# A spectral filter ahead of expert routing: the first two batches' last stage fed through DRAM instead of through transposes

## The chip, the cores and the metric

The kernel runs on one core of a Trainium2 chip. The metric is the device time of one execution in microseconds (us). A core has a matrix engine (TensorE, "PE" in the profile; "PEld" are its weight loads), VectorE (DVE), ScalarE (ACT), GpSimd (POOL) and a sync engine (SP) that issues most of the transfers. "SPq" and "ACTq" are the instruction queues of SP and ACT as issuers of DMAs. Each engine works through its instructions in the order in which the program issued them.

## The reference

All data is float32. `x` has 8 batches of 2496 tokens with 256 channels.

```python
X = np.fft.rfft(x, axis=1)
Y = X * (filt_r + 1j * filt_i)[None]
y = np.fft.irfft(Y, n=2496, axis=1)            # (8, 2496, 256)
t = y.reshape(19968, 256)
expert = token_ids * 2654435761 % 8
for e in range(8):
    rows = expert == e
    out[rows] = np.maximum(t[rows] @ w1[e], 0) @ w2[e]   # w1: 256 x 1024, w2: 1024 x 256
```

## The kernel before

**Two halves.** The transform along the 2496 = 39 x 64 tokens is made of matmuls, batch by batch. The second half gathers the filtered tokens by expert into tiles of 256 rows and runs each tile through its expert's two layers. A token of the first half is put to its place by a scatter: `stage3` copies its result into a tile `o` of 117 rows, and POOL issues one indirect DMA for each column of `o`, 22 for a batch, into the DRAM array `xs`. The tiles are loaded from `xs`. The first tiles hold tokens of batches 0 and 1, so they wait for every scatter of these two.

**The stages of a batch.** `stage1` is the 39-point transform: matmuls of `x` with the table `wf_t`, six steps of four columns (`u` = 0 to 5, the last one half as large). `forward` multiplies the result, in 20 planes of 128 partitions, two planes a step and so ten steps, by the table `d_t` and then, on VectorE, by the filter. `back` multiplies by the table `e_t`. `stage3` is the inverse 39-point transform with `wi_t`, again six steps of four columns, followed by four scatters a step (two in the last). `room` fills the columns of `o` that hold the token number. Between stages the data must change its partitions.

From batch 2 on it does so through DRAM: `stage1` stores to `d1`, `load2` loads from it, `back` stores to `d2`, `load4` loads from that. The first two batches differ. The first has no trip at all before its `forward` (`stage1_c`, `turn2`). And both of them have a `back_c` (L373) that makes the output with channels on the partitions, written into the buffer `self.out`, and a `turn4` (L382), which transposes this on TensorE, 44 transposes a batch, into the tile `t4` that `stage3` reads. The copies out of PSUM are ScalarE's for the first batch and VectorE's for the second.

**Buffers.** `self.out` of the first batch is the front part of `wts`, which later holds the weights of tiles 0 and 1 (`weights(0, .)` the first half of it, `weights(1, .)` the second). That of the second batch is `mid[:, 5:10]`, whose parts also serve as `stage1` output of the fourth batch. `t4` has two buffers, the tile `o` four (two pools, taken in turn), the input tiles `x` two; PSUM has four general banks (`fps`, tag "f") and four with names, a to d.

**The order.** The schedule is written by hand. Every piece of work is a pair of a number and a function; `todo` is sorted by the number, and the pieces are issued in that order. The numbers are roughly microseconds but they only order: nothing waits for a clock. `head` is the list of all that is issued before the first expert tile: batches 0 and 1 entirely, `stage1` of batch 2 (`third`) and two thirds of `stage1` of batch 3 (`fourth`), the routing, and the weights of tiles 0 and 1. The pieces of the later batches are issued between the steps of the expert tiles.

On SP's queue before the change stand, in this order: `load2` of the second batch (four of five groups), `load2` of the fifth, the third batch's x, the weights of tiles 0 and 1, the fourth batch's x, and then the first loads from `xs`. The third batch's `stage1` steps stand between the `turn4` and `stage3` steps of the second batch, the fourth's come after all of these:

```python
head += [(96 + 5 * u - 4 * (u > 0), lambda u=u: second.turn4(u)) for u in range(NU)]
head += [(98 + 5 * u, lambda u=u: second.stage3(u)) for u in range(NU)]
head += [(99 + 5 * u - 3 * (u == 5), lambda u=u: third.stage1(u)) for u in range(NU)]
head += [(123 + .1 * u, lambda u=u: fourth.stage1(u)) for u in range(4)]
```

Of the kernel before, what the change touches and what calls it, by code (L numbers as in the profile page):

```python
# [11 lines left out]
F32 = mybir.dt.float32  # L12
# [7 lines left out]
P = 128  # L20
B, S, C = 8, 2496, 256
# [8 lines left out]
NS, NQ = N1 // 2 + 1, 64  # L30
H, HN = 3, 21
H0 = (2 * HN, 0, HN)
NR = H * N1
NK = 2 * H * NS
SG = 4
XG = 4
NU = (HN + XG) // XG
XL = 2 * XG
# [87 lines left out]
def kernel(  # L126
# [10 lines left out]
    nc = tc.nc  # L137
# [17 lines left out]
    dpool = pool(ctx, "dram", 2, DRAM)  # L155
# [3 lines left out]
    t4pool = pool(ctx, "t4", 2)  # L159
    opool = pool(ctx, "op", 2)  # L160
    fps = pool(ctx, "fps", 4, PSUM)
    banks = {k: pool(ctx, f"bank_{k}", 1, PSUM) for k in "abcd"}

    ident = keep.tile([P, P], F32)
# [8 lines left out]
    e_t = cpool.tile([P, NS, P], F32)  # L173
# [45 lines left out]
    class Batch:  # L219


        def __init__(self, b):
            self.b = b
            self.d1 = self.d2 = None
            self.x, self.t2, self.t4, self.p, self.o = {}, {}, {}, {}, {}
            self.g = None
            if b < 2:

                if b == 0:
                    own = mid[:, 0:5, :].rearrange("p k f -> p (k f)")  # L230
                    self.mixed = own.rearrange("p (h n s) -> p h n s", h=2, s=NS)
                after = (held[:, 0:NS * C] if b == 0 else mid[:, 5:10, :].rearrange("p k f -> p (k f)"))
                self.out = after.rearrange("p (h n s) -> p h n s", h=2, s=NS)

        def load1(self, v):

# [16 lines left out]
        def products(self, w, rows, cols, src, dst, copy, u, name):  # L253


            last = XG * u + XG > HN
            for i in range(1 if last else XG // 2):
                ps = fps.tile([P, 2, C], F32, name=f"{name}_{self.b}_{u}_{i}", tag="f")
                if last:
                    for k, f in enumerate((H, 1)):  # L260
                        nc.tensor.matmul(out=ps[0:cols * f, k, :], lhsT=w[0:rows[k], 0:cols * f],
                                         rhs=src[0:rows[k], k, :], start=True, stop=True)
                    for k, f in enumerate((H, 1)):
                        copy(out=dst[0:cols * f, k, 0:C], in_=ps[0:cols * f, k, :])
                else:
                    for k in range(2):
                        nc.tensor.matmul(out=ps[0:cols * H, k, :], lhsT=w[:], rhs=src[:, 2 * i + k, :],  # L267
                                         start=True, stop=True)
                    copy(out=dst[:, 2 * i:2 * i + 2, 0:C], in_=ps[0:cols * H])  # L269
# [100 lines left out]
            self.t2[u] = held[:, a:a + 2 * C].rearrange("p (i c) -> p i c", c=C)  # L370
            nc.scalar.copy(out=self.t2[u], in_=ps[:])

        def back_c(self, u):  # L373
            pr = self.p.pop(u)
            ps = fps.tile([P, 2, 2, P], F32, name=f"pc_{self.b}_{u}", tag="f")
            for i in range(2):
                for h in range(2):
                    nc.tensor.matmul(out=ps[:, i, h, :], lhsT=pr[:, i, h * P:(h + 1) * P],
                                     rhs=e_t[:, 2 * u + i, :], start=True, stop=True)
            nc.scalar.copy(out=self.out[:, :, :, 2 * u:2 * u + 2], in_=ps[:].rearrange("p i h n -> p h n i"))  # L380

        def turn4(self, u):  # L382
            v, j0 = divmod(XG * u, XL)
            if j0 == 0:
                self.t4[v] = t4pool.tile([NK, XL, C], F32, name=f"t4_{self.b}_{v}", tag="t4")
            copy = nc.vector.tensor_copy if self.b else nc.scalar.copy
            for k in range(0, min(XG, HN + 1 - XG * u), 2):
                tag = ("bc" if self.b and u % 2 else "ad")[k // 2]
                ps = banks[tag].tile([P, 2, C], F32, name=f"pu_{self.b}_{u}_{k}", tag=tag)
                rows = [2 * NS * (H if XG * u + k + i < HN else 1) for i in range(2)]  # L390
                for i in range(2):
                    n0 = 2 * H * (XG * u + k + i)
                    for h in range(2):
                        nc.tensor.transpose(out=ps[0:rows[i], i, h * P:(h + 1) * P],
                                            in_=self.out[:, h].rearrange("p n s -> p (n s)")[:, n0 * NS:n0 * NS + rows[i]],
                                            identity=ident[:])
                if rows[0] == rows[1]:
                    copy(out=self.t4[v][:, j0 + k:j0 + k + 2, :], in_=ps[0:NK])
                else:
                    for i in range(2):  # L400
                        copy(out=self.t4[v][0:rows[i], j0 + k + i, :], in_=ps[0:rows[i], i, :])

        def load4(self, v):
            self.t4[v] = t4pool.tile([NK, XL, C], F32, name=f"t4_{self.b}_{v}", tag="t4")
# [36 lines left out]
    first, second = batches[:2]  # L441
# [307 lines left out]
    N_2 = NS // 2  # L749

    def chain(k):

        for step, j in ((Batch.turn2, k + 1), (Batch.back_c, k - 2), (Batch.forward, k)):
            if 0 <= j < N_2:
                step(first, j)

# [6 lines left out]
    third = batches[2]  # L763
# [10 lines left out]
    head += [(30.1, lambda: nc.sync.dma_start(out=wi_t[:], in_=wi_dram.ap()))]  # L774
    head += [(t, lambda u=u: second.stage1(u)) for u, t in enumerate((27, 32, 38, 41, 45, 48.5))]
    head += [(15, places), (64, tile_experts), (70, experts), (118, blanks)]
    head += [(t, lambda g=g: second.load2(g)) for g, t in enumerate((54, 54.1, 54.2, 54.3, 70))]
    head += [(62.7 + 2.9 * u, lambda u=u: second.forward(u)) for u in range(N_2)]
    head += [(62.7 + 2.9 * (u + 2) - .1, lambda u=u: second.back_c(u)) for u in range(N_2)]
    at = (63, 68.6, 74.4, 80.2, 86, 91)  # L780
    head += [(t, lambda u=u: first.room(u)) for u, t in enumerate((60, 65, 71, 77, 83, 88.5))]
    head += [(t, lambda u=u: second.room(u)) for u, t in enumerate((92, 96.9, 101.9, 106.9, 111.9, 116.9))]
    head += [(t, lambda u=u: first.turn4(u)) for u, t in enumerate(at)]
    head += [(t + 3, lambda u=u: first.stage3(u)) for u, t in enumerate(at)]
    head += [(t, lambda v=v: third.load1(v)) for v, t in enumerate((72, 73, 74))]
    head += [(t, lambda k=k: weights(k // 2, k % 2)) for k, t in enumerate((95, 95.1, 95.2, 95.3))]
    head += [(96 + 5 * u - 4 * (u > 0), lambda u=u: second.turn4(u)) for u in range(NU)]
    head += [(98 + 5 * u, lambda u=u: second.stage3(u)) for u in range(NU)]
    head += [(99 + 5 * u - 3 * (u == 5), lambda u=u: third.stage1(u)) for u in range(NU)]
    head += [(123.5, lambda: begin()), (123.6, lambda: [load(i) for i in range(2)])]  # L790
    head += [(124, lambda: [nc.sync.dma_start(out=dram, in_=chip) for dram, chip in put_off[2]])]
    head += [(125 + .1 * g, lambda g=g: third.load2(g)) for g in range(4)]
    fourth = batches[3]
    head += [(126, lambda: [nc.sync.dma_start(out=dram, in_=chip) for dram, chip in put_off[3]])]
    head += [(t, lambda v=v: fourth.load1(v)) for v, t in enumerate((113, 113.1))]
    head += [(123 + .1 * u, lambda u=u: fourth.stage1(u)) for u in range(4)]
    todo = [(t - 200, piece) for t, piece in head]
    todo += [(t, lambda k=k: pads(k)) for k, t in enumerate((10.9, 11.6, 11.9, 16.9, 17.6, 17.95, 22.9))]

# [331 lines left out]
```

## Time and profile before

| | |
|---|---|
| median of 3 runs | 1425.08 us (1418.89 to 1428.87) |
| the profiled execution | 1424.24 us, its span 1422.5 us |
| mean granted TensorE clock | 0.99 |
| first matmul of the first expert tile | 141.85 us from the span's start |
| last scatter of the second batch issued | 135.26 us |
| scatters (POOL, L433) in the whole kernel | 176, of 1006 ns on average |
| stage 3 matmuls `pd` (L267) in the whole kernel | 320, of 385 ns |

The span is the time from the first to the last recorded instruction. In a line of a timeline, the first column is the start, the second the duration from the first to the last of the merged instructions, then come engine, source line, operation, output and input, shapes, the count, and in brackets the idle time of the engine before it with what ended it. In the chain of waits, each line is a start, a duration and what was being waited for or done. A line of a table by stretches has, for each engine, the busy time and in brackets the number of instructions, and at the end the granted clock, the DMA engines' busy share and the GB/s. Busy times of TensorE are modelled ends of pipelined matmuls: a group of 8 that is listed with 1.89 us comes every 1.73.

### The profile page before, as it was taken

To read this page: it belongs to the slowest core of one execution; us is meant where nothing else is said; L and a number is where in the kernel's file an instruction comes from. 1 tells how busy PE (TensorE), PEld (TensorE's weight loads), DVE (VectorE), ACT (ScalarE), POOL (GpSimd) and SP (SyncE) were. 2 spreads that over 40 slices of the span, in tenths; PEclk is the share of its full clock that TensorE was granted. 3 is DMA by queue.
4 is the path that set the end of the run, shared out by engine and by line. 5 is a ranking of instruction groups with operands and counts; after the bars stand their busy time and mean duration, and the time that the engine had idled before them with its cause. 6 is when DMAs were issued, how large, how long until landed. Compare 5 with 4: busy or idle time off the path is not lost.

```text
span 1422.5 us, 26307 instructions
## 1 busy us (share of the span) xinstructions
PE 1373.4 (97%) x9398; PEld 1273.3 (90%) x9398; DVE 890.2 (63%) x1636; ACT 416.6 (29%) x760; POOL 830.3 (58%) x736
## 2 busy tenths in 40 slices
PE   7898999999999999999999999999999999999997
PEld 7776888989888988889999899999999999999997
DVE  7773575575556566445665477657766776676775
ACT  4554122223232223232222222222222222222222
POOL 6167243844665565578533587788855566555563
PEclk9999899999999999999999999999999999999999
DMA  8677765757987698888755785887742526261611
GB/s 222 206 235 216 212 218 121 260 192 245 269 270 224 183 284 264 261 262 273 241 167 131 219 258 170 235 242 235 254 138 68 190 62 199 46 218 42 215 46 35
DMA packets 244505, 278.33 MB, mean 196 GB/s; under 512 B 125171, under 2 KB 213670, under 8 KB 234948
## 3 DMA queue, kind: packets, MB, share of 16 engines
q1 hardware_dynamic: 95149, 179.33, 40.2%
q10 hardware_dynamic: 129303, 52.69, 15.4%
q0 software_dynamic: 19920, 44.59, 8.9%
q8 instruction: 77, 1.26, 0.4%
q14 instruction: 56, 0.46, 0.1%
HBM read 293.65 MB, written 86.15 MB: 267 GB/s over the span
## 4 chain that ended last, share of the span: by engine, by line
PE 86%; DMA 8%; DVE 3%; issue 1%; ACT 1%; ACTq 0%; SPq 0%; POOLq 0%; POOL 0%; DVEq 0%
PE dps L922 22%; PE up_b L887 9%; PE up_a L887 6%; PE up_c L887 6%; PE pd L267 5%; PE pb L312 4%; PE dnc L949 4%; PE dnb L949 4%; PE dna L949 4%; PE upc L944 4%; PE upa L944 4%; PE pc L335 3%; PE pa L267 3%; DMA t<-d 2%; PE upe L944 2%; PE upb L944 2%
## 5 line engine op out<-in xcount | busy, mean ns | idle before, releaser
L922 PE MATMUL dps<-wts,ht 128*128 128x256 f32 x1600 | 370.9, 382 | 6.1 <-ACT ht L891 6.1
L922 PEld LDWEIGHTS dps<-wts,ht 128*128 128x128 f32 x1600 | 304.7, 192 | 50.6 <-ACT ht L891 7.3
L1014 POOL DMA_INDIRECT out_dram<-osb,no x158 | 165.2, 1046 | 219.2 <-DVE osb L956 137.8
L433 POOL DMA_INDIRECT xs<-o,sidx x176 | 177.0, 1006 | 168.7 <-ACT o L269 73.3
L877 POOL TENSOR_TENSOR tw<-wts 128x512 f32<-128x512 f32 x158 | 205.1, 1298 | 116.0 <-DMA wts<-in_moe_w_dram 92.4
L877 POOL TENSOR_TENSOR tw<-wts,tw 128x512 f32<-128x512 f32 x158 | 206.1, 1305 | 6.2
L894 DVE TENSOR_TENSOR ht<-up_b,ht 128x512 f32<-128x512 f32 x150 | 103.7, 691 | 114.6 <-PE up_b L887 91.2
L891 ACT ACTIVATE ht<-ht 128x512 f32<-128x512 f32 x150 | 94.3, 630 | 188.8 <-DVE ht L894 164.9
L322 DVE TENSOR_TENSOR z<-pb,filt 64x512 f32<-64x512 f32 x160 | 110.2, 689 | 30.9 <-PE pc L335 28.9
L927 DVE COPY osb<-dps 128x512 f32<-128x512 f32 x50 | 34.6, 691 | 150.2 <-PE dps L922 149.7
L887 PE MATMUL up_a<-xt,wts 128*128 128x128 f32 x800 | 115.3, 277 | 9.1 <-DVE xt L855 4.9
L887 PEld LDWEIGHTS up_a<-xt,wts 128*128 128x128 f32 x800 | 105.9, 193 | 12.7 <-DVE xt L855 5.3
L887 PE MATMUL up_b<-st,tw 128*128 128x128 f32 x800 | 107.4, 278 | 2.7 <-DVE ht L894 1.8
L887 PEld LDWEIGHTS up_b<-st,tw 128*128 128x128 f32 x800 | 98.1, 193 | 4.9 <-issue 3.7
L953 ACT ACTIVATE ht<-ht 128x512 f32<-128x512 f32 x90 | 56.6, 630 | 122.1 <-DVE ht L956 75.8
L894 DVE TENSOR_TENSOR ht<-up_c,ht 128x512 f32<-128x512 f32 x100 | 69.0, 690 | 37.2 <-PE up_c L887 32.4
L338 ACT COPY mid<-pc 128x512 f32<-128x512 f32 x60 | 35.0, 584 | 154.8 <-PE pc L335 91.5
L267 PE MATMUL pd<-t,wi_t 120*117 120x256 f32 x320 | 77.5, 385 | 2.6 <-DMA t<-d 2.6
L318 DVE TENSOR_TENSOR y<-pb,filt 128x512 f32<-128x512 f32 x80 | 55.1, 689 | 37.8 <-PE pb L312 35.6
L269 ACT COPY o<-pd 117x512 f32<-117x512 f32 x80 | 45.0, 585 | 104.4 <-DMA xg<-xs 45.4
L312 PE MATMUL pb<-mid,d_t 128*128 128x256 f32 x280 | 74.1, 388 | 1.1 <-DVE z L322 1.1
L898 ACT COPY ht<-up_a 128x512 f32<-128x512 f32 x50 | 29.3, 587 | 150.6 <-PE up_a L887 120.7
(210 smaller groups left out, 2466.1 us busy)
## 6 DMA issues: line engine op xcount, KB each, us to landing
wts<-in_moe_w_dram SPq DMA_DIRECT2D x162, 1024.0 KB
xg<-xs ACTq DMA_DIRECT2D x321, 64.0 KB
mid<-d SPq DMA_DIRECT2D x70, 256.0 KB
d<-mid ACTq DMA_DIRECT2D x60, 256.0 KB
d_t<-t2s SPq DMA_DIRECT2D x15, 1024.0 KB
e_t<-t2s SPq DMA_DIRECT2D x15, 1024.0 KB
x<-in_x_dram SPq DMA_DIRECT2D x39, 312.0 KB
t<-d SPq DMA_DIRECT2D x12, 960.0 KB
```

Of the source, the lines that this page charges most:

```text
L267: nc.tensor.matmul(out=ps[0:cols * H, k, :], lhsT=w[:], rhs=src[:, 2 * i + k, :], start=True, stop=True)
L312: nc.tensor.matmul(out=ps[:, i, :], lhsT=d_t[:, s, :], rhs=rhs, start=True, stop=True)
L322: nc.vector.tensor_tensor(out=z[b], in0=ps[a], in1=f_t[1][64 * hi:64 * hi + 64, s1:s1 + 2, :], op=OP.mult)
L433: st = nc.gpsimd.indirect_dma_start(out=xs[:], out_offset=bass.IndirectOffsetOnAxis(ap=index, axis=0), in_=rows, in_offset=None, bounds_ch ...
L877: eng.tensor_tensor(t[k][:], p, q, op=OP.subtract)
L887: nc.tensor.matmul(out=ps[bank][:, f, :], lhsT=w[:, f * P:(f + 1) * P], rhs=xx, start=first and f == 0, stop=True, skip_group_check=True)
L891: nc.scalar.activation(out=out, in_=in_, func=AF.Relu)
L894: nc.vector.tensor_tensor(out, ps[bank][:], other, op=OP.add)
L922: nc.tensor.matmul(out=ps[:, h, :], lhsT=ht[:, h, fp, :], rhs=w2[:, fp, :], start=(fp == 0), stop=(fp == FP - 1))
L944: nc.tensor.matmul(out=ps[:, f, :], lhsT=w[:, f * P:(f + 1) * P], rhs=xx, start=first and f == 0, stop=True, skip_group_check=True)
L949: nc.tensor.matmul(out=ps[:, 0, :], lhsT=a[:, f, :], rhs=b[:, f, :], start=first and f == 0, stop=True, skip_group_check=True)
L1014: st = nc.gpsimd.indirect_dma_start(out=out[:], out_offset=bass.IndirectOffsetOnAxis(ap=to_rows[i][:, h:h + 1], axis=0), in_=o[:, h, :], i ...
```

## The change

For the first two batches `turn4` and `back_c` go. `back_on_chip` keeps the output in planes, as `back` does for later batches, and copies it into the same buffer `self.out`. `put` stores a fifth of it (four planes, 128 partitions x 4 KB) to a DRAM tile `d2`, right after the second `back_on_chip` of each fifth, and `fetch` loads a third of the columns from `d2` into the tile `t4` for `stage3`. Both are issued on SP. The first `fetch` of a batch follows its last `put` at once. `stage3` of the two batches uses the PSUM banks a to d.

The order in `head` is written anew. On SP now stand, one after another: four `put` of the first batch with four `load2` of the second ahead of the fifth `put`; `fetch` 0 and 1; the last `load2`; the third batch's x; `put` 0 of the second batch; the first batch's `fetch` 2; `put` 1; `weights(0, .)`; `put` 2, 3, 4; `fetch` 0 and 1 of the second batch; `fetch` 2; `weights(1, .)`; the fourth batch's x. On TensorE the third batch's `stage1` is issued about the end of the second batch's `back_on_chip` (four of its six steps after the last one, ahead of `stage3`(0)), and the fourth's steps between the `stage3` steps of the second.

```diff
             for i in range(1 if last else XG // 2):
-                ps = fps.tile([P, 2, C], F32, name=f"{name}_{self.b}_{u}_{i}", tag="f")
+                tag = ("bc" if u % 2 else "ad")[i] if name == "pd" and self.b < 2 else "f"
+                ps = (fps if tag == "f" else banks[tag]).tile([P, 2, C], F32, name=f"{name}_{self.b}_{u}_{i}", tag=tag)
...
-        def back_c(self, u):
+        def back_on_chip(self, u):
             pr = self.p.pop(u)
-            ps = fps.tile([P, 2, 2, P], F32, name=f"pc_{self.b}_{u}", tag="f")
+            ps = fps.tile([P, 2, C], F32, name=f"pc_{self.b}_{u}", tag="f")
             for i in range(2):
-                for h in range(2):
-                    nc.tensor.matmul(out=ps[:, i, h, :], lhsT=pr[:, i, h * P:(h + 1) * P],
-                                     rhs=e_t[:, 2 * u + i, :], start=True, stop=True)
-            nc.scalar.copy(out=self.out[:, :, :, 2 * u:2 * u + 2], in_=ps[:].rearrange("p i h n -> p h n i"))
-
-        def turn4(self, u):
...
+                nc.tensor.matmul(out=ps[:, i, :], lhsT=e_t[:, 2 * u + i, :], rhs=pr[:, i, :], start=True, stop=True)
+            nc.scalar.copy(out=self.out[:, 2 * u:2 * u + 2, :], in_=ps[:])
+
+        def put(self, k):
+
+            if self.d2 is None:
+                self.d2 = dpool.tile([P, NS, C], F32, name=f"d2_{self.b}", tag="d2")
+            sl = slice(SG * k, SG * k + SG)
+            nc.sync.dma_start(out=self.d2[:, sl, :], in_=self.out[:, sl, :])
+
+        def fetch(self, v):
+            t4 = self.t4[v] = t4pool.tile([NK, XL, C], F32, name=f"t4_{self.b}_{v}", tag="t4")
+            n = min(XL, HN - XL * v)
+            main = self.d2[0:2 * H * HN].rearrange("(j x) s c -> (x s) j c", x=2 * H)
+            nc.sync.dma_start(out=t4[:, 0:n, :], in_=main[:, XL * v:XL * v + n, :])
+            if n < XL:
+                nc.sync.dma_start(out=t4[0:2 * NS, n, :], in_=self.d2[2 * H * HN:P].rearrange("x s c -> (x s) c"))
...
-        for step, j in ((Batch.turn2, k + 1), (Batch.back_c, k - 2), (Batch.forward, k)):
+        for step, j in ((Batch.turn2, k + 1), (Batch.back_on_chip, k - 2), (Batch.forward, k)):
...
-    head += [(t, lambda g=g: second.load2(g)) for g, t in enumerate((54, 54.1, 54.2, 54.3, 70))]
+    head += [(t, lambda g=g: second.load2(g)) for g, t in enumerate((55.5, 55.6, 55.7, 55.8, 66))]
...
-    head += [(62.7 + 2.9 * (u + 2) - .1, lambda u=u: second.back_c(u)) for u in range(N_2)]
-    at = (63, 68.6, 74.4, 80.2, 86, 91)
-    head += [(t, lambda u=u: first.room(u)) for u, t in enumerate((60, 65, 71, 77, 83, 88.5))]
-    head += [(t, lambda u=u: second.room(u)) for u, t in enumerate((92, 96.9, 101.9, 106.9, 111.9, 116.9))]
-    head += [(t, lambda u=u: first.turn4(u)) for u, t in enumerate(at)]
-    head += [(t + 3, lambda u=u: first.stage3(u)) for u, t in enumerate(at)]
-    head += [(t, lambda v=v: third.load1(v)) for v, t in enumerate((72, 73, 74))]
-    head += [(t, lambda k=k: weights(k // 2, k % 2)) for k, t in enumerate((95, 95.1, 95.2, 95.3))]
-    head += [(96 + 5 * u - 4 * (u > 0), lambda u=u: second.turn4(u)) for u in range(NU)]
-    head += [(98 + 5 * u, lambda u=u: second.stage3(u)) for u in range(NU)]
-    head += [(99 + 5 * u - 3 * (u == 5), lambda u=u: third.stage1(u)) for u in range(NU)]
+    head += [(62.7 + 2.9 * (u + 2) - .1, lambda u=u: second.back_on_chip(u)) for u in range(N_2)]
+    head += [(69 + 4.4 * u, lambda u=u: first.room(u)) for u in range(NU)]
+    head += [(70.5 + 4.4 * u, lambda u=u: first.stage3(u)) for u in range(NU)]
+    head += [(t, lambda v=v: first.fetch(v)) for v, t in enumerate((62.66, 62.67, 75.5))]
+    head += [(23 + 3.6 * (2 * k + 3) + .05, lambda k=k: first.put(k)) for k in range(NS // SG)]
+    head += [(t, lambda v=v: third.load1(v)) for v, t in enumerate((66.1, 66.2, 66.3))]
+    head += [(t, lambda k=k: weights(k // 2, k % 2)) for k, t in enumerate((77.2, 77.3, 104.2, 104.3))]
+    head += [(97 + 4.1 * u, lambda u=u: second.room(u)) for u in range(NU)]
+    head += [(98.5 + 4.1 * u, lambda u=u: second.stage3(u)) for u in range(NU)]
+    head += [(t, lambda v=v: second.fetch(v)) for v, t in enumerate((94.56, 94.57, 103))]
+    head += [(62.7 + 2.9 * (2 * k + 3) - .05, lambda k=k: second.put(k)) for k in range(NS // SG)]
+    head += [(t, lambda u=u: third.stage1(u)) for u, t in enumerate((89.5, 92, 94.6, 95, 95.1, 95.2))]
...
-    head += [(t, lambda v=v: fourth.load1(v)) for v, t in enumerate((113, 113.1))]
-    head += [(123 + .1 * u, lambda u=u: fourth.stage1(u)) for u in range(4)]
+    head += [(t, lambda v=v: fourth.load1(v)) for v, t in enumerate((104.4, 104.5))]
+    head += [(107.5 + 4.1 * u, lambda u=u: fourth.stage1(u)) for u in range(4)]
```

More of the change, by code (lines that the diff above doesn't have):

```diff
@@ L232, in __init__ @@
                 after = (held[:, 0:NS * C] if b == 0 else mid[:, 5:10, :].rearrange("p k f -> p (k f)"))
-                self.out = after.rearrange("p (h n s) -> p h n s", h=2, s=NS)
+                self.out = after.rearrange("p (s c) -> p s c", c=C)
         def load1(self, v):
@@ L382, in turn4 @@
-        def turn4(self, u):
[L383 to L401, printed above, removed]
```

## The prediction

> **What bounds the kernel now.** I read the page first, for the engine that is full.
>
> ```profile
> PE 1373.4 (97%) x9398; PEld 1273.3 (90%) x9398; DVE 890.2 (63%) x1636; ACT 416.6 (29%) x760; POOL 830.3 (58%) x736
> ```
>
> TensorE is busy 97% of the span, so work taken off it seems worth its own time. But the change touches the head alone, the stretch before the expert tiles begin. So I read the chain of waits in order of time where the head meets the first tile:
>
> ```profile
> 138.46 2.31 DMA xg<-xs
> ...
> 141.08 0.72 DVE xt L855
> 141.85 2.08 PE up_a L887 x8
> ```
>
> The first tile's matmul (141.85) waits for a transpose of the rows `xg`, these for a load out of `xs`, and that load for the last scatter into `xs`. The waits of SP's own queue say so too ("SPq L844 <- DMA xs<-o,sidx", 11.4 us). So what matters is when the scatters end. They are POOL's, and its timeline shows their pace:
>
> ```profile
> 101.86 0.99 POOL L433 DMA_INDIRECT xs<-o,sidx  x1 [0.30 <-issue]
> 103.15 0.99 POOL L433 DMA_INDIRECT xs<-o,sidx  x1 [0.30 <-issue]
> 104.44 0.90 POOL L433 DMA_INDIRECT xs<-o,sidx  x1 [0.30 <-issue]
> 105.70 0.99 POOL L433 DMA_INDIRECT xs<-o,sidx  x1 [0.36 <-ACT o L269]
> ...
> 122.55 1.00 POOL L433 DMA_INDIRECT xs<-o,sidx  x1 [0.31 <-issue]
> 126.09 1.00 POOL L433 DMA_INDIRECT xs<-o,sidx  x1 [2.55 <-ACT mid L269]
> ...
> 135.26 0.90 POOL L433 DMA_INDIRECT xs<-o,sidx  x1 [0.30 <-ACT mid L269]
> ```
>
> That last line is what SP waited for. One scatter every 1.295 us, whatever TensorE does: 22 of them for a batch take 21 x 1.295 + 0.95 = 28.15 us. From 97.78 to 136.16 POOL has one hole, 2.55 us at 123.55. The first batch's last scatter ends at 105.34, the second's first begins at 105.70. **From there the head is bound by POOL**, and TensorE's work beside it is free. Third, the DMAs, by stretches:
>
> ```profile
> 73.00:86.00 13.00, 10.63 (x67) 9.22 (x67) 11.21 (x28) 5.59 (x10) 6.51 (x7) 1.00 0.85 295
> 86.00:98.00 12.00, 12.00 (x80) 10.85 (x79) 11.02 (x19) 7.02 (x13) 7.70 (x9) 1.00 0.60 173
> 98.00:112.00 14.00, 13.22 (x83) 11.10 (x82) 5.58 (x12) 7.29 (x15) 10.77 (x11) 1.00 0.96 307
> ```
>
> The last two columns are the engines' DMA share and GB/s. 295 GB/s at 0.85 and 307 at 0.96 put the ceiling for this mixture near 330; there is room at 86 to 98, none after.
>
> **What the Trainium skill says.** "DMA: Bandwidth & Descriptors", the section on the anatomy of one DMA, gives each DMA a fixed cost of about 2 us, mostly the receipt of its last write. The trace agrees: a 64 KB piece of `xg` took 2.31 us. The section on queues, rings and completion order of the same page says that a sequencer's DMAs pass each DMA engine in ring order, and that the engines take turns between rings. No view of the kernel before tests it; I use it for what `put` and `fetch` queue behind on SP. "TensorE: Matmul & The Clock Gate", in its steps of a matmul, says that matmuls stay in program order, so one that waits holds all behind it; its Part 1 halves the clock after an idle window of about 3.4 us. Here 8 matmuls of `pd` took 3.26 us at 240.26 after a pause, 1.89 us otherwise.
>
> **Part by part.** *Removed.* `turn4`:
>
> ```profile
> 101.92 1.96 PE L394 MATMUL pu<-ident,mid 128*120 128x128 f32 x16 [0.78 <-ACT mid L380]
> 103.71 1.89 PE L267 MATMUL pd<-t,wi_t 120*117 120x256 f32 x8
> 105.44 1.89 PE L267 MATMUL pa<-x,wf_t 117*120 117x256 f32 x8
> 107.17 1.04 PE L394 MATMUL pu<-ident,mid 128*120 128x128 f32 x8
> ```
>
> Starts differ by 0.87 us a group, so 5.5 groups a batch are 4.8 us, 9.6 us of TensorE for two, and 6.0 us of ACT (first batch) and 7.2 us of DVE (second) in copies. All of it lies beside DVE's filter products (2.87 us for each of ten steps) or POOL's scatters: worth nothing to the end. `back_on_chip` swaps 8 matmuls of 0.89 us in all for 4 of 0.86: nothing. The `pd` tags only give it other PSUM banks: nothing.
>
> *First batch's trip through DRAM.* `back` 9's copy ends at 65.04. SP's ring then holds `put` 3 (0.52 MB) and four `load2` (2.10 MB), issued from 59.3 and carried before at 275 to 356 GB/s till about 67.5. `put` 4 (0.52 MB) comes behind: data until 70.5, landed 71.6. `fetch` 0 (0.98 MB) costs 2.3 us fixed and 2.9 of data, 5.2. `stage3`(0), at 68.00 before, starts at 77. Its scatters are not late in the end (first at 79, POOL then continuous to 107.5), but in TensorE's queue `forward` 3 stands behind it. DVE has products until 76.9 and gets the next at 80.4: the second batch's chain is 3.5 us late.
>
> *DMAs until the second batch's last `put`.* SP's ring carries from 73 on: `fetch` 0 and 1 1.97 MB, `load2`(4) 0.52, the third's x 2.64, `put` 0 to 3 2.10, `fetch` 2 0.66, `weights`(0) 2.10, together 9.98 MB. Beside it a scatter moves 0.12 MB in 1.295 us, 94 GB/s, from 79 to 107.5. At 330 GB/s in all: 6 us x 0.33 + 28.5 x 0.236 = 8.7 MB by 107.5. The last `put`'s copy is ready at 105 to 107: ten filter steps from 80.4 on and `back` 9, which is queued behind `stage1`(1) of the third and `stage3`(5). So 1.8 MB remain with that `put` and are landed at 113, beside 0.98 MB of the third's `d1` on ACT's ring. `fetch` 0 adds 5.2: `stage3`(0) at **118** instead of 103.71, first scatter at 120.0. Bounds: 113.8, when the ring is empty and the trip is two fixed costs and the data (105 + 3.85 + 5.2), and 124, at 310 GB/s with the `d1` store ahead. POOL has nothing between 107.5 and 120. With 28.15 us for 22 scatters they end at 148.1, against 136.16: +12.0, the old hole counted.
>
> *The fourth's `stage1` among them.* `stage1`(0) of the fourth stands before `stage3`(3) on TensorE. Its x is issued on SP behind `fetch` 2, which waits for the tile that `stage3`(1) reads (3.5 us after the start), and behind `weights`(1): 0.66 + 2.10 + 0.96 = 3.7 MB at 330 less 94 GB/s are 15.7 us, so it lands some 20 us after the start. With 2 to 3 us for cold matmuls, and 2 to the next scatter, that is 24; POOL wants it at 2 + 12 x 1.295 = 17.5. Price 6.5; bounds 0 (x is there in time) and 9. I take 5, for the scatters cease when POOL runs dry and leave the DMAs to x.
>
> *Moved at no cost.* The third's `stage1`, 9.6 us of TensorE, fits in the 11 us between `back` 9 and the fetched tile; if that is short, it would be late by the rest. `weights`(0) goes ahead, `weights`(1) is not read before the second tile. `room` only waits on DVE, where nothing is behind it. After the last scatter all is as before: 5.7 us to the first matmul, with the clock down either way.
>
> **Sum.** 12 + 5 = 17 us. The profiled execution took 1424.24 us (span 1422.5 and 1.7 around it), 0.84 below the median 1425.08 of three. 1424.24 + 17 = **1441 us**, 1.1% above the median.
>
> **Rivals.** (a) *Two holes but no hold of the fourth's x, and a ring that keeps up*: `stage3`(0) at 114 to 115, +8 to +9: 1433. For it: 0.60 share at 86 to 98. Against: ten more MB in the head. (b) *The DMAs jam*: the fetched tile at 124 and the hold at 9: +18 + 9 = 27, 1451. For it: an `xs` landing took up to 9.6 us before, and in the main loop a store and its fetch took 5.45 + 11.78 us. Against: the head has no tile loads. (c) *Not slower*: the second batch's trip is short. It decides at a first scatter of 105.70 + 2.24 = 108, since POOL then ends where it did, without its hole. For that the first's fetch must land by 72, so that DVE never waits, `back` 9 must be copied by 100, and the put and fetch take 6 us: first scatter 107, 1423. For it: the quiet SP ring. Against: two fixed costs alone are 4.6 us and the data 4.4. (d) *TensorE was the limit after all*, its 9.6 us count: 1415. Against: POOL's unbroken row.
>
> **How the numbers follow.** Forecast 0.50, (a) 0.27, (b) 0.13, (c) 0.07, (d) 0.03. Some 1% (14 us) is what a measurement of this kernel can tell from no change. The forecast reaches from +12 to +22, over the line (+14.2) in four fifths of it; (b) is over it, (a) in a tenth: slower 0.55. Faster by over 1% would need more than POOL's 44 scatters leave: 0.04 is generous; the rest 0.41. Range: from (a)'s low edge, 1427, to (b)'s, 1454; (c) and (d) and the worst of (b) are left out. The forecast's own range is 1436 to 1446.
>
> **What would show it.** POOL: scatters at 1.295 us to about 107, a hole of 8 to 13 us, a second hole after the twelfth scatter of the second batch. TensorE: waits on `t<-d` at about 70 and 112, and on `x` after the third `stage3` of the second batch. The first `up_a` near 159. It is wrong if the second batch's first scatter comes before 112, or if `up_a` starts under 150.

## The result, and the profile after

The changed kernel took 1462.26 us (median of 4 runs, 1456.99 to 1468.39), the kernel before 1422.59 us beside it: a ratio of 1.0276, 95% interval 1.0216 to 1.0335. It is slower by about 40 us where the forecast said 17, and outside the range. The profiled execution took 1464.55 us, its span 1462.8 us; the execution profiled before took 1424.24, so the two traces differ by 40.3 us.

Where those 40 us arise can be read from a single pair of numbers. The first expert tile's `up_a` starts at 182.24 instead of 141.85, so 40.4 us are lost before it and nothing after it. The engine table and two groups of the page already say what kind of loss it is (busy time, mean, and after the second bar the idle time ahead of the group, with what ended it):

```profile
PE 1368.2 (94%) x9230; PEld 1262.8 (86%) x9230; DVE 877.6 (60%) x1624; ACT 407.9 (28%) x748; POOL 827.7 (57%) x736
...
L426 POOL DMA_INDIRECT xs<-o,sidx x176 | 175.8, 999 | 208.2 <-ACT o L270 131.8
...
L268 PE MATMUL pd<-t,wi_t 120*117 120x256 f32 x320 | 80.4, 397 | 21.9 <-DMA t<-d 21.9
...
L268 PE MATMUL pa<-x,wf_t 117*120 117x256 f32 x264 | 65.5, 394 | 21.6 <-DMA x<-in_x_dram 21.6
```

TensorE is busy 5.2 us less and the kernel is 40 us longer: the transposes that went were worth nothing to the end. In their place TensorE stands 21.9 us for `t<-d`, the fetched tile (2.6 before), and 21.6 us for `x`. POOL's timeline shows how both reach the scatters:

```profile
86.36 1.10 POOL L426 DMA_INDIRECT xs<-o,sidx  x1 [39.26 <-ACT o L270]
...
118.79 0.90 POOL L426 DMA_INDIRECT xs<-o,sidx  x1 [0.30 <-DVE o L405]
136.25 0.99 POOL L426 DMA_INDIRECT xs<-o,sidx  x1 [16.56 <-ACT o L270]
...
150.48 0.99 POOL L426 DMA_INDIRECT xs<-o,sidx  x1 [0.30 <-issue]
163.90 0.99 POOL L426 DMA_INDIRECT xs<-o,sidx  x1 [12.43 <-ACT o L270]
...
175.55 0.89 POOL L426 DMA_INDIRECT xs<-o,sidx  x1 [0.30 <-issue]
```

The first batch's scatters begin at 86.36 (69.97 before) and end at 119.7. POOL is then empty for 16.56 us; the second batch begins at 136.25 instead of 105.70, which is 30.55 us. After the twelfth scatter a second hole, 12.43 us; each scatter between comes at the old pace of about 1.29 us. The hole of 2.55 us of before is gone. Less the 0.30 us that stand before every scatter, 30.55 + 12.13 - 2.25 = 40.4, the whole difference.

The chain of waits tells what stands behind each hole (start, duration, what was done or waited for):

```profile
35.83 16.02 DMA d<-mid
...
67.74 1.12 PE pc L378 x4
68.88 0.59 ACT wts L379
69.49 5.73 DMA d<-wts
75.37 7.96 DMA t<-d
83.33 0.04 issue
83.37 3.65 PE pd L268 x8
...
93.96 11.88 DMA t<-d
105.83 0.04 issue
105.88 2.44 PE pd L268 x8
...
117.68 0.59 ACT mid L379
118.30 7.22 DMA d<-mid
125.62 0.04 issue
125.67 7.56 DMA t<-d
133.22 0.04 issue
133.27 6.04 PE pd L268 x16
...
146.56 11.71 DMA x<-in_x_dram
158.27 0.14 issue
158.40 3.67 PE pa L268 x8
```

Read it as a row of trips. (The first line is the second batch's store to `d1`.) First batch: last copy 68.88, put 5.73 us, fetch 7.96, and stage 3's first eight matmuls at 83.37 with a cold clock, 3.65 us for what comes every 1.73 otherwise. Then its third fetch, issued at 93.96, holds stage 3 again until 105.88. Second batch: last copy 117.68, put 7.22, fetch 7.56, stage 3 at 133.27. Last the fourth's x, landed at 158.27. DVE's timeline shows what the first batch's two holds did to the second batch's filter products:

```profile
88.79 0.69 DVE L319 TENSOR_TENSOR y<-pb,filt 128x512 f32<-128x512 f32 x1 [8.03 <-PE pb L313]
...
111.31 0.69 DVE L319 TENSOR_TENSOR y<-pb,filt 128x512 f32<-128x512 f32 x1 [4.93 <-PE pb L313]
```

Twice DVE waits for `pb`, 8.03 and 4.93 us, since `forward` stands behind a waiting `stage3` in TensorE's order. That makes the second batch late before its own trip begins.

### The profile page after: what moved, and what is told of

Read it like the earlier page. It is cut to its first block, busy times and chain, and to the rows that moved or that the text cites. A ratio compares the mean times of both kernels' runs of the same rounds, so it can differ in the third digit from the quotient of the medians.

```text
span 1462.8 us, 25961 instructions
## 1 busy us (share of the span) xinstructions
PE 1368.2 (94%) x9230; PEld 1262.8 (86%) x9230; DVE 877.6 (60%) x1624; ACT 407.9 (28%) x748; POOL 827.7 (57%) x736
## 4 chain that ended last, share of the span: by engine, by line
PE 82%; DMA 10%; DVE 4%; issue 1%; ACT 1%; SPq 1%; ACTq 0%; POOL 0%; POOLq 0%; DVEq 0%
PE dps L916 21%; PE up_b L881 8%; PE up_a L881 6%; PE up_c L881 5%; PE pd L268 5%; DMA t<-d 4%; PE dnc L943 4%; PE dna L943 4%; PE dnb L943 4%; PE pb L313 4%; PE upc L938 4%; PE upa L938 4%; PE pc L336 3%; PE pa L268 3%; DMA xg<-xs 2%; DMA d<-mid 2%
## 5 line engine op out<-in xcount | busy, mean ns | idle before, releaser
L268 PE MATMUL pd<-t,wi_t 120*117 120x256 f32 x320 | 80.4, 397 | 21.9 <-DMA t<-d 21.9
L268 PEld LDWEIGHTS pd<-t,wi_t 120*117 120x117 f32 x320 | 60.0, 191 | 35.3 <-DMA t<-d 23.8
L268 PE MATMUL pa<-x,wf_t 117*120 117x256 f32 x264 | 65.5, 394 | 21.6 <-DMA x<-in_x_dram 21.6
```

## The experiments

Except where told, each kernel is the changed one with a small edit, and all but 7 and 12 keep the edit of the first. "Ratio" is to the kernel before, measured beside it. That took 1422 to 1423 us beside 1 to 4 and 13 to 15, and 1455 to 1457 beside 5 to 12; why isn't known, and no trace of it was taken there. In the traces of 5 to 12 what follows the first `up_a` is longer (1294 to 1312 us, 1275 to 1282 in the others), and each has waits of 2 to 20 us of TensorE, DVE or ACT in the head for which the profile names no cause, where the others have none over 2 us. Some stand where the changed kernel's trace names one. So a ratio of 5 to 12 doesn't measure the head alone, and a small difference there shows no cause.

**1. The fourth's `stage1` behind the last `stage3`.** The second hole by itself.

```diff
-    head += [(107.5 + 4.1 * u, lambda u=u: fourth.stage1(u)) for u in range(4)]
+    head += [(123 + .1 * u, lambda u=u: fourth.stage1(u)) for u in range(4)]
```

> The changed kernel with the fourth batch's stage1 steps issued after the second batch's last stage3, as in the kernel before; its loads stay where the change put them. Theory H (a queued matmul that waits for x holds stage3, and POOL runs dry): the 12.1 us hole in the scatters at 152 us goes, the 22 scatters of the second batch run at 1.295 us from 136 on, first tile matmul near 170 us, 1450 us (1446 to 1453). Rival J (the DMAs are jammed by the added 10 MB, and the scatters' own landing is what stops POOL there): a hole of 6 us or more stays, 1456 or more.

1455.57 us, ratio 1.0234 (1.0180 to 1.0287). The timeline of TensorE:

```profile
158.00 10.09 PE L268 MATMUL pa<-x,wf_t 117*120 117x256 f32 x32 [11.20 <-DMA x<-in_x_dram]
171.59 1.65 PE L881 MATMUL up_a<-xt,wts 128*128 128x128 f32 x6 [3.50 <-DVE xt L849]
```

The 22 scatters run unbroken from 135.57, the last at 162.80 (12.75 earlier); `up_a` comes 10.65 earlier, since the fourth's `stage1` now stands right before the tiles and costs 2.1 there. The medians differ by 6.7, the profiled executions by 9.6; 1455.57 is above the expected 1446 to 1453. The hole was the hold of the fourth's x, and only a part of it came back in time.

**2. The changed order, but with the transposes for both batches** (`back_c` and `turn4` as before; no `put`, no `fetch`; `turn4`(u) ahead of `stage3`(u); the edit of 1). Three more things return toward the kernel before: the third's `stage1` stands between the second's `stage3` steps, these begin at 94.58 instead of 98.5, and `weights(0, .)` moves from 77.2 to 92.1.

```diff
-    head += [(t, lambda v=v: second.fetch(v)) for v, t in enumerate((94.56, 94.57, 103))]
-    head += [(62.7 + 2.9 * (2 * k + 3) - .05, lambda k=k: second.put(k)) for k in range(NS // SG)]
+    head += [(94.55 + 4.1 * u, lambda u=u: second.turn4(u)) for u in range(NU)]
+    head += [(94.58 + 4.1 * u, lambda u=u: second.stage3(u)) for u in range(NU)]
...
```

> Transposes for both batches again, with the change's new spacing of the first batch's stage3 (4.4 apart) and of the second's (4.1), the third batch's stage1 between the second's stage3 steps and the fourth's after them. Theory T (both trips through DRAM make the loss, the new order does not): first scatter of the second batch at 104 to 108 us, no long hole, 1421 us (1416 to 1427). Rival O (the new order of loads and stages costs by itself): over 1435.

1423.57 us, ratio 1.0011 (0.9986 to 1.0037).

```profile
108.16 0.99 POOL L457 DMA_INDIRECT xs<-o,sidx  x1 [1.64 <-ACT o L271]
```

That is the second batch's first scatter, and its only hole; `up_a` at 142.31. So this order neither helps nor hurts: **without the trips through DRAM there is no loss.** The change's own place for the third's `stage1`, ahead of the second's `stage3`, wasn't tested alone. In the changed kernel these steps end at 123.8, and TensorE then stands 9.45 us for the fetched tile, so there they cost the end nothing.

**3 and 4. One trip each.** The same, with the transposes for the first batch alone (3), so that only the second batch goes through DRAM, and for the second alone (4).

> Transposes for the first batch only; the second goes through DRAM as in the change; the fourth's stage1 late. Theory T: VectorE is no longer held for the first batch's fetches (8.0 and 4.9 us) nor by the puts at 41 to 64 us, so the last back step of the second batch is copied at 102 to 105 and its trip costs 14.8 us: first scatter of the second batch at 119 to 122, 1435 us (1430 to 1441). Rival J (jam by the amount of traffic): half of the added traffic is gone, so about half of what is left in a_fourth_late against before, 1436, but with slow puts and fetches and the copy of the last back step still after 110.

> The first batch through DRAM as in the change, the second by transposes; the fourth's stage1 late. Theory T: VectorE is held as in the change (last back step copied near 118), but its trip is gone: first scatter of the second batch near 121 us, 1437 us (1431 to 1442). Rival P (the first batch's trip hides behind its own scatters, only the second's trip counts): first scatter of the second batch by 110, 1427 or less.

The second's trip alone: 1438.40 us, ratio 1.0122 (1.0065 to 1.0178). The first's alone: 1434.78, 1.0085 (1.0060 to 1.0110). Added, 28.7 us of the 33.4 that both cost in experiment 1. In the head, where less else varies, `up_a` comes at 158.92 and 155.86, 17.1 and 14.0 us after 141.85; together 31.1, against 29.7 in experiment 1. So they are about additive, and neither is harmless. Chain of the kernel with the second's trip:

```profile
100.78 11.06 DMA d<-mid
111.83 0.02 issue
...
111.90 2.60 DMA d<-mid
...
114.62 7.70 DMA t<-d
```

Here the second's last `back` copy is ready at 102.8, 1 us after the kernel before, and the first batch's own last copy ends at 64.95 instead of 69.47: without the first's puts the second batch's store to `d1`, issued at 34.46, had landed by 47.69 (13.2 us; 12.5 in the kernel before, 16.0 in the changed one). From 66 us on no filter product waits longer for `pb` than this one:

```profile
91.94 0.69 DVE L320 TENSOR_TENSOR y<-pb,filt 128x512 f32<-128x512 f32 x1 [0.99 <-PE pb L314]
```

So the holds of 8.03 and 4.93 us came with the first's trip, and without it the second's last copy is ready 15.5 us earlier than in the changed kernel (118.3). The put's 2.60 us are about what one transfer costs alone, but it was issued 9 us after its data were ready. SP stood 12.5 us for a landing "DMA d<-mid" that is not its data: the program's instruction list gives all transfers of SP and ACT eight completion semaphores in rotation, and this put shares one with ACT's store of the third batch eight transfers earlier, issued at 100.78. A ninth transfer isn't issued before the first of the eight has landed. And with the first's trip alone:

```profile
90.31 1.10 POOL L457 DMA_INDIRECT xs<-o,sidx  x1 [42.06 <-ACT o L271]
```

From there POOL has no hole over 1 us, yet it began 20 us late: the last of 44 scatters is issued at 149.07, 13.8 after before. **A trip costs the head even where it makes no long hole**, because the first batch's slack is used up, the four holes among its scatters in the kernel before (7.7 us in all):

```profile
77.88 0.99 POOL L433 DMA_INDIRECT xs<-o,sidx  x1 [2.89 <-ACT o L269]
...
85.54 0.99 POOL L433 DMA_INDIRECT xs<-o,sidx  x1 [2.38 <-ACT o L269]
...
91.66 0.99 POOL L433 DMA_INDIRECT xs<-o,sidx  x1 [1.24 <-ACT o L269]
...
97.78 1.00 POOL L433 DMA_INDIRECT xs<-o,sidx  x1 [1.23 <-ACT o L269]
```

**5. No landing to wait for.** Stand-in: `fetch` reads rows of x with the same shape, not what was put; the puts stay.

```diff
-            main = self.d2[0:2 * H * HN].rearrange("(j x) s c -> (x s) j c", x=2 * H)
+            main = bass.AP(tensor=x.tensor, offset=x.offset + self.b * S * C,
+                           ap=[[C, NK], [2 * H * NS * C, HN], [1, C]])
```

> a_fourth_late with fetch reading rows of x, in the same pieces of 1 KB at the same distances, in place of what put stored: no fetch waits for a put to land, all DMAs stay, the output is not the reference's. Theory L (the landing of the last put is 5 to 7 us of each trip): the first stage3 starts at 78 to 79 instead of 83.9, the second batch's at 121 to 124 instead of 132.6, 1446 us (1442 to 1450). Rival B (the bytes take that time anyway, landing or not): starts within 2 us of a_fourth_late's, 1452 or more.

Ratio 1.0137 (1.0086 to 1.0188). The first's `stage3` starts at 78.51, 5.4 earlier than in experiment 1, but the second's at 132.12, 0.5 earlier: its fetch, issued at 121.02 right behind the last put, takes 11.1 us with the put's bytes ahead of it. The starts mislead, since the second's last copy ended later here (120.59, 117.20 in experiment 1), behind waits without a named cause. From last copy to `stage3` the first batch took 11.0 us, against 14.5 in experiment 1 and 14.7 in 7, and the second 11.5, against 15.4 and 15.3. So the landing was worth 3.5 to 3.9 us of either trip, and some 11 us stay without it. The ratio says nothing of this, `up_a` being at 179.00.

**6. Long pieces.** The same stand-in with 8 KB in a row instead of 1 KB.

> e_no_landing with each partition of a fetch read from x as one piece of 8 KB instead of eight of 1 KB; the output is not the reference's. Theory W (a fetch runs at some 200 GB/s because of its 1 KB pieces): fetch 0 takes 2.4 us less in each batch, both holds of TensorE end that much earlier, 1441 us, 4 to 5 under e_no_landing. Rival: the rate comes from the 120 partitions or from other traffic, equal to e_no_landing within 2 us.

Ratio 1.0175 (1.0139 to 1.0210). Fetch 0 still took 9.2 us (70.42 to 79.58) and 12.4 us (118.12 to 130.57), against 10.4 and 11.1 in experiment 5. Both have a put's bytes ahead of them, so this gives no sign that the piece size makes the fetch slow, and no clean test of it.

**7. The fourth's x ahead of `fetch` 2 and `weights(1, .)`**, its `stage1` among the `stage3` steps as in the change.

```diff
-    head += [(t, lambda v=v: fourth.load1(v)) for v, t in enumerate((104.4, 104.5))]
+    head += [(t, lambda v=v: fourth.load1(v)) for v, t in enumerate((94.58, 95.3))]
```

> The changed kernel, the fourth's stage1 between the second's stage3 steps as there, but its x issued right after the second batch's fetch 0 and 1, ahead of fetch 2 and weights(1). Theory H (only the late landing of x makes the second hole): x lands by 143 us, no hole of over 2 us in the second batch's scatters, 1454 us (1450 to 1457), level with a_fourth_late. Rival (the fourth's stage1 between them costs by its own TensorE and ScalarE time): a hole of 5 us or more stays, 1459 or more.

Ratio 1.0183 (1.0136 to 1.0230). TensorE waits 0.73 us for x instead of 17.38, and POOL's second hole is

```profile
162.66 0.99 POOL L426 DMA_INDIRECT xs<-o,sidx  x1 [3.15 <-ACT o L270]
```

3.15 instead of 12.43, and before the fifth step, the one that needs `fetch` 2, instead of the fourth. The order of SP's queue made the long hole. What makes the short one isn't shown: TensorE began that step's matmuls at 151.96, ScalarE's copies of them came only at 161.77, and ScalarE's wait of 2.95 us before these has no named cause.

**8. The first's `stage3` moved back, so that `forward` isn't held** (`stage3` at 79 + 3.6 u, its `fetch` 2 at 83).

> a_fourth_late with the first batch's stage3 steps issued later (79 + 3.6 u instead of 70.5 + 4.4 u), so that forward 3 to 5 of the second batch stand ahead of the first of them on TensorE. Theory Q (TensorE's queue, not the data, holds VectorE for 8 us): no idle time of over 3 us on VectorE before the fourth filter step, last back copy of the second batch at 108 to 111 instead of 117, first scatter of the second batch at 127 to 130, 1447 us (1443 to 1451). Rival B (the ring of DMAs sets the second trip): first scatter of the second batch unchanged at 134 to 136, 1453 or more.

Ratio 1.0262 (1.0229 to 1.0296), no better than 1. DVE's filter products were not held, but SP was (second column: from the first to the last of the merged issues):

```profile
94.97 2.14 SPq L457 DMA_DIRECT2D wts<-in_moe_w_dram  x2
117.39 0.44 SPq L460 DMA_DIRECT2D wts<-in_moe_w_dram  x1
...
118.55 0.43 SPq L392 DMA_DIRECT2D t<-d  x1
```

The third load of the weights stood 19.5 us for "DMA d<-mid", a shared semaphore again, ACT's store of the third batch, with `fetch` 2 of the first batch behind it; TensorE waited 26.92 us for that tile. A part of the 19.5 us is that ACT issued that store only at 111.35. So the test didn't answer its question.

**9 and 10. The weights behind the second's fetches** (9: `weights` 0 and 1 at 104.2 to 104.35, the fourth's x at 103.1), and that with the move of 8 (10).

> a_fourth_late with weights(0) moved from ahead of put 2 to behind the second batch's fetch 2 (and the fourth's x ahead of all weights). Theory R (2.1 MB of weights in SP's ring delay the second batch's last put and the third's d1 store beside it): last back copy at 115 to 117 as there, put 4 landed in 3 to 4 us instead of 7, first scatter of the second batch at 131 to 132 instead of 135.6, 1.020 of the kernel before (1.0234 there). Rival (the ring is empty by then): first scatter at 135 to 136, 1.0234.

> n_weights_last with the first batch's stage3 steps issued later (79 + 3.6 u) and its fetch 2 at 83, so that forward 3 to 5 of the second batch stand ahead of the first stage3 on TensorE. Theory Q (the place in TensorE's queue holds VectorE, 8.0 and 4.9 us): no wait of VectorE of over 3 us before the second batch's fourth filter step, last back copy at 107 to 110, first scatter of the second batch 7 to 8 us earlier than in n_weights_last, 1.0145. Rival (the fetched data come so late that some other step takes the wait): less than 3 us earlier, 1.018 or more.

Ratios 1.0262 (1.0234 to 1.0291) and 1.0225 (1.0197 to 1.0254). In 9, 2.1 MB less in front of the last put didn't make it faster: 6.88 us, 7.15 in experiment 1. The copy itself came later, at 121.99 instead of 116.61, with 7.82 us without a named cause on DVE before it. So the theory that the weights delay that put isn't borne out. In 10 no filter product of the second batch waits over 2.2 us, and TensorE's timeline has

```profile
131.51 8.72 PE L268 MATMUL pd<-t,wi_t 120*117 120x256 f32 x32 [10.02 <-DMA t<-d]
```

The last of these products ends at 98.58 (119.03 in 9, 114.13 in the changed kernel): it was the order on TensorE that held them. Not all of that arrives. The second's last copy ends at 113.93, only 8.1 us earlier than in 9: steps of `stage3` that were moved back now come in front of `back`, and TensorE stood 4.97 us before one of them (no cause is named; its tile's fetch had been issued at 96.00). And the last put leaves only at 119.6: ahead of it on SP a piece of the first's `fetch` 2 stood until 118.77 for ACT's store of the third batch, again by a shared semaphore. The second's `stage3` starts 6.0 us earlier than in 9 (137.50) and `up_a` 6.8 earlier (173.85 against 180.64). The ratio missed its forecast of 1.0145, and what the hold of `forward` is worth by itself isn't sized here, since 9 has that unnamed wait.

**11. One fetch less** (the second's `fetch` 1 left out and its tile zeroed, so a third of that batch isn't loaded).

> a_fourth_late without the second batch's fetch 1, whose tile is set to zeros on VectorE; the output is not the reference's. Theory S (fetch 0 takes 8 us because fetch 1, issued 0.5 us later, shares the DMA engines with it): fetch 0 lands 5.0 to 5.8 us after its issue, first scatter of the second batch at 133, 1.0217 of the kernel before. Rival W (a fetch alone moves at 200 GB/s): 7.0 us or more, first scatter unchanged, 1.0234.

Ratio 1.0210 (1.0179 to 1.0240). Fetch 0 alone took 6.9 us (124.79 to 131.7), against 7.56 to 8.04 with a neighbour: sharing explains up to 1 us of the 2.4 that it took over the prediction.

**12. The kernel before, closer.** To use what was learnt: transposes kept, the first batch's `turn4` and `stage3` every 4.8 instead of 5.6, the routing of tiles after the filter products, x of the third and half of the weights elsewhere.

```diff
-    at = (63, 68.6, 74.4, 80.2, 86, 91)
+    at = (63, 67.8, 72.6, 77.4, 82.2, 87)
```

> The kernel before, still with transposes: the first batch's turn4 and stage3 4.8 apart instead of 5.8, the first forward of the second batch ahead of the last back step of the first, the routing's small VectorE steps behind the filter steps, third's x earlier, weights(1) later. Theory T (the end of the head is the second batch's first scatter plus 28 us of scatters): VectorE's filter steps end at 95 to 96 instead of 99.4, first scatter of the second batch at 101 to 103 instead of 105.7, no hole, first tile matmul at 137 to 139, 4 us less: 0.997. Rival (TensorE is full there and takes it back): 105 or later, 1.000.

Ratio to the kernel before 1.0076 (1.0047 to 1.0105), slower. The second's first scatter came at 123.61 (105.70), after a hole of 9.11 us. The forecast was 101 to 103. Why the steps put closer made it later isn't shown: ACT once stood 6.76 us and DVE 4.74 us without a named cause. No version here beats the kernel before.

**13 to 15. Is it the shared semaphore?** One store to `d1` is issued by POOL, whose transfers have other semaphores: the second batch's first (13 on experiment 1, 14 on the kernel before), the third's first (15, on experiment 3).

```diff
-                    nc.scalar.dma_start(out=dram, in_=chip)
+                    (nc.gpsimd if (self.b, v) == (1, 0) else nc.scalar).dma_start(out=dram, in_=chip)
```

> Edit, on top of the first experiment (the fourth's stage 1 behind the last stage 3): the store of the second batch's stage-1 output of its first third to d1 is issued by POOL, which is idle then, and no longer by ACT. In the program's list of instructions ACT's next store signals on the same completion semaphore, eight transfers later, and so can't be issued before the first one has landed; in the changed kernel ACT stands 6.0 us for that, with the first batch's copies behind it. Theory S (it is this wait that makes the first batch late): ACT's wait is gone, the first batch's last back copy ends near 64 instead of 68.3, its first stage 3 starts near 79 to 80 instead of 83.9, the first tile's matmul 3 to 4.5 us earlier than 171.59 of the first experiment's clock, a ratio near 1.0205 against 1.0234 there. Theory D (the store's data are what is late: the second batch's loads and the first's puts share the DMA engines): the last back copy within 1.5 us of 68.3 and the ratio as before, 1.0225 to 1.0245.

> Edit on the kernel before: the same store by POOL. There ACT stands 2.39 us for it (filter copy at 47.84). Theory S: that idle time goes, the first batch's last back copy comes up to 2.4 us earlier (62.8 before), the first tile's matmul 1 to 2.4 us earlier: a ratio of 0.998 to 0.9995. Theory D, or DVE's filter products being the bound there: nothing moves, 1.000.

> Edit on the kernel with the transposes for the first batch alone: the third batch's store of its first third to d1 is issued by POOL, no longer by ACT. In that kernel the fifth put of the second batch was ready at 102.8 and was issued at 111.90, since it signals on the same semaphore as ACT's store issued at 100.78, eight transfers before. Theory S: the put is issued at 103 to 104 and has landed by 109, the first stage 3 of the second batch starts at 115 to 118 instead of 122.36, its first scatter at 118 to 121 instead of 125.34, the first tile's matmul 4 to 7 us before 158.92; ratio near 1.008 against 1.0122. Theory D (the put shares the engines with the store's 0.98 MB and lands no earlier): the put lands at 112 or later, the fetched tile at 120 or later, the ratio 1.011 to 1.0125.

13: 1.0272 (1.0226 to 1.0319); 14: 1.0033 (1.0014 to 1.0052). Both miss. ACT's next store went out at 45.23 instead of 51.93, but POOL, which works in order too, issued the moved one only at 48.5, behind its transfers for the routing, and ACT then stood 6.84 us for the buffer `mid` that this store reads. What ACT's wait costs by itself stays open. 15: ratio 1.0112 (1.0067 to 1.0158).

```profile
104.18 7.28 DMA d<-mid
111.58 9.25 DMA t<-d
```

The put is issued 7.7 us earlier, though the last copy came 1.4 later (104.16), and lands 3 earlier; it takes 7.28 us instead of 2.60. The fetch behind it takes 9.25 instead of 7.70, and the second's first scatter comes at 123.85 instead of 125.34. So of the 9.1 us that the put had stood, 2.9 came back, counted from the copy. **The wait that could be seen was not the whole cost: with it gone, the transfers behind it took longer.** The test isn't pure, since POOL issued the moved store only at 104.83, 4 us later than ACT had and right beside the put. The ratios, 1.0112 and 1.0122, can't be told apart.

## Why the prediction was right in kind and wrong in size

*Right.* POOL's scatters bound the head, TensorE's 5 us bought nothing, two holes appeared where they were named, the second batch's chain was late because `forward` stood behind `stage3`, and the tail from the last scatter to `up_a` stayed (5.8 us, 5.7 before). Rival (c), a short trip, and (d), TensorE, are refuted by the result: the first scatter came at 136.25, and 5.2 us less of TensorE made nothing faster. By experiments 1 and 2 the trips alone cost some 33 us once the hole of x is taken away. Rival (b), jammed DMAs, came nearest in number (a fetched tile at 124 and a hold of 9; measured 133.3 and 12.1), but most of what the forecast missed in the first arose before the last put, where TensorE and DVE stood for the first batch's fetches, and (b) did not have that.

*Wrong.* The sum was 17 and the head lost 40.4. The 23.4 us between them sit in three terms.

First, **when the second batch's last copy is ready: 117.7 to 118.3, not 105 to 107.** The step "the second batch's chain is 3.5 us late" was mis-sized, in parts that each looked small. The first's last copy ended at 69.47, not 65.04: with its own puts beside it the second batch's store to `d1` takes longer, and I had charged their bytes only after 65 (without them, experiment 3, it ended at 64.95). The put was 0.8 quicker than priced, but the fetch took 7.96, not 5.2, and the first group of matmuls, cold, 3.65, not 1.9. That makes DVE's next product 88.79 instead of 80.4, 8.4 us. Then the first's `fetch` 2 held TensorE and DVE a second time, 4.93 us on DVE; it was counted among SP's bytes and nowhere as a wait. Together 13.3 us, against the 12.3 by which the copy was later than forecast. Experiment 3 shows that they come from the first batch's trip: without it the last copy ends at 102.80.

Second, **the fetch: 7.56 us, not 5.2.** I had divided its bytes by 330 GB/s, the ceiling of a mixture. By stretches:

```profile
106.00:118.00 12.00, 12.00 (x47) 9.40 (x48) 3.38 (x9) 5.64 (x11) 6.54 (x7) 0.86 0.97 360
...
126.00:134.00 8.00, 0.73 (x2) 0.63 (x3) 0.17 (x1) 0.00 (x0) 0.00 (x0) 0.61 0.86 179
```

In the second stretch the fetches are alone and the engines are busy 0.86 of the time, but move 179 GB/s, where the mixture before it moves 360. The put, priced at about 7, took 7.2. So the first scatter is at 136.25 instead of 120.0, 16.25 of the missing 23.4: some 12.3 from the copy (118.3 against the middle of 105 to 107), 2.4 from the fetch, and the rest, 1.6, from the put, the landing and the cold start.

Third, **the second hole: 12.1 us beyond the pace, not 5.** The other 7.1. The prediction priced the hold of x at 6.5 and took 5, since POOL's dry scatters would leave the DMAs to x. SP's own timeline shows why x was late all the same:

```profile
125.67 13.97 SPq L392 DMA_DIRECT2D t<-d  x3
...
141.68 1.32 SPq L457 DMA_DIRECT2D wts<-in_moe_w_dram  x2
143.19 0.51 SPq L460 DMA_DIRECT2D wts<-in_moe_w_dram  x1
143.74 5.93 SPq L249 DMA_DIRECT2D x<-in_x_dram  x6
```

The third `fetch` waits until 139.3 for the tile that the cold `stage3`(1) reads, 6 us after the start and not 3.5; x is issued at 143.74, lands 25 us after the start instead of 20, and its own matmuls are cold (3.67 us). The bound of 9 left that out.

Of what the prediction took from the Trainium skill, the order on TensorE ("TensorE: Matmul & The Clock Gate", the steps of a matmul) is what the traces show: matmuls stayed in order, and those behind a waiting one were held. The clock's halving after an idle window of about 3.4 us (its Part 1) fits in part: eight matmuls took 3.65 to 3.77 us after waits of 5 to 27 us. But the example of the kernel before, 3.26 us at 240.26, came after a wait of only 2.04 us, and other waits of some 2 us were followed by 1.96 to 3.60, so 3.4 us isn't a limit that these traces confirm. The fixed cost of about 2 us ("DMA: Bandwidth & Descriptors", the anatomy of one DMA) is given there for transfers issued by GpSimd, and those of the trip are SP's; for them this case has 2.60 us for the put that ran nearly alone in experiment 3. What failed was the bytes per second that I put beside it.

## What to carry to other kernels

A trip through DRAM in the middle of a chain has to be priced as landing plus fetch plus a cold restart, each from a transfer of that very shape, and once more for every instruction that stands behind the waiting one on an in-order engine. Lateness that one batch hands to the next adds up: take the time at which the last producer is ready from a walk through all holds, not from the old schedule plus the first of them. Before you take away a wait that the profile names, ask what bytes lie behind it: the wait can go and most of the time stay.

## What was not expected of the hardware and the program

- A load of 0.98 MB from DRAM into 120 partitions took 6.9 us alone and 7.6 to 8.0 beside its neighbour, with 1 KB pieces; 8 KB pieces, in a busier ring, were no quicker. If some 2 us of it are fixed (a 64 KB load took 2.31), the data moved at about 200 GB/s (an estimate: 0.98 MB in 4.9 us). Why so slow stays open.
- Transfers of SP and ACT share eight completion semaphores in rotation, so a transfer can stand for one of another queue: 9 us in experiment 3, and up to 19.5 in experiment 8, where that other transfer was itself issued late. Where it was taken away (15), 2.9 of 9 us came back; the store that was moved then left beside the put.
- A store issued by POOL instead of ACT stands in POOL's order: 48.5 us against 35.8.
